# A scheduler's durations refitted, its plan told of two shared PSUM banks, and a rank written out for each of its tasks

## The chip, the cores and the metric

The kernel runs on one core of one Trainium2 chip. The core has five engines with queues of their own: TensorE (PE in the profile, PEld its weight loads), VectorE (DVE), ScalarE (ACT), GpSimd (POOL) and SyncE (SP), which here issues nearly all DMA transfers. Each engine takes its instructions strictly in the order in which they were written into the program and waits on semaphores for what others must have done. The metric is the device time of one execution in microseconds; three runs of the kernel before gave a median of 870.45.

## The reference

An attention block without softmax, with a root-mean-square norm of each head, feeds a two-layer network with softplus:

```python
kv = einsum('bhsd,bhse->bhde', k, v)          # q, k, v: 8 x 8 heads x 576 x 64
out = einsum('bhsd,bhde->bhse', q, kv)
x = out / sqrt(mean(out * out, -1) + 1e-6) * g_norm    # then laid out as 4608 tokens x 512
h = x @ w_in                                   # 512 x 2048
g = log(1 + exp(h))                            # written so that it does not overflow
y = g @ w_out                                  # 2048 x 512; y is 4608 x 512
```

The weights come as 64-bit floats, q, k and v as 32-bit floats.

## The kernel before

**What is computed where.** TensorE multiplies in a 32-bit format that keeps fewer bits than the inputs have, so each operand of the two large products is split into a high part and smaller parts, three pieces in all, and each product is the sum of three matmuls per 128 rows of the contraction. The splitting is ScalarE and VectorE work: for a tile of x, `high` on ACT (L635), `low` (L638) and `less` (L641) on DVE; for the softplus output, L882, L869 and L873 in the first stage and L1117, L1120, L1123 in the later ones.

**The head.** Each 512 KB piece of a 64-bit weight is loaded by SP (L418), turned into 32-bit floats by one ACT instruction (L429) and six DVE instructions (`high1` L433, `high2` L437, `mask` L442, `power` L450, `rest` L455, `total` L459), and split (`low` is L503 or L506, `low_up` L509). For the first four chunks of 128 hidden units the third piece is made with a pair of matmuls (L520 and L521). Meanwhile K and V of the eight batches are loaded (L680, L678) and multiplied in groups of 8 matmuls of 64 columns (L691); q tiles are turned by PE (L771) or, from the third batch, by DVE (L746); an output group (L715, 16 matmuls) makes 128 tokens of attention output; ACT squares them (L788), DVE sums (L719), POOL takes the inverse root with two instructions (L722, L723), DVE scales (L727); the tile is turned by PE (L733) and split into x pieces for block products. Tokens are numbered in 36 tiles of 128, tiles 0 to 2 are block 0, and so on for 12 blocks. The outputs of the attention are also stored to DRAM (L798, L818) and loaded again later (L836, `x_again`). The trace records a group of 32-bit matmuls with two records for each matmul (so the 8 matmuls of L691 stand as x16, the 16 of L715 as x32).

**The first stage.** For each block of 384 tokens and each of the first four or six chunks, a *product* (L858, `mm1`, 12 matmuls of 384 columns) makes the hidden units, ACT applies softplus (L880), ACT and DVE split it, and three groups of three matmuls (L865, `mm2`) add to three sums in PSUM. Attention work is put between these groups until about 300 us.

**The wide stages.** The rest of the hidden units is done in two passes over nine blocks of 512 tokens, two chunks at a time, with seven products (L1060, 6 matmuls of 256 columns) in place of eight. These feed on each other: copies by ACT in PSUM (L1101, L1105, `c1` and `c6` in `wide_step`) stand between a product and a later one that adds to its copy. The second layer is L1130, three matmuls of 512 columns for each of eight places. Sums leave PSUM by ACT (L925), go to DRAM as parts, and come back to be added by DVE (L904).

**What sets the order.** Nothing is ordered by hand. `kernel` creates 3,795 tasks with `add(engine, ns, run, after, pos, take, give, ...)`: an engine, a duration, what must be done before, a position `pos` and the buffers that are taken and given back. `Plan.order` then plays the program: it keeps a clock for each engine and one for the DMA, adds a hand-over time after each task, and again and again takes the task that can start first. Among tasks of one engine that could start within `SOON` (150 ns) of the first, the one with the smallest `pos` wins; PE has rules that keep 64-wide matmuls (kinds `rows` and `kv`) together. The result, sorted by planned start, is the order in which the instructions are written. The chip then runs that order; the planned times themselves are thrown away. `plan.spare` is a filler: where PE would be idle in the plan before the seventh product, a matmul without use (L1224) is put in, 52 in all. `pos` comes from formulas with 179 written numbers (`P0` to `P7`).

```python
at, t = min(options, key=lambda o: (o[1].pos, o[0]))
...
t.start = at
engine_free[t.engine] = at + t.ns
t.end = at + t.ns + self.HANDOVER[t.engine]
```

The buffers `o` (two halves spread over two PSUM banks) and `tp` (one bank) are used by PE, ACT and DVE in turns; the program makes an engine wait until another is done with a bank.

## Time and profile before

| | |
|---|---|
| three runs | 869.46, 870.45 (median), 872.05 us |
| the profiled execution, first to last instruction | 867.5 us; the page gives no other time for it |
| first product L858 starts | 44.44 us |
| last matmul starts | 863.3 us |
| PE busy, of which fillers L1224 | 853.9 us, 18.9 |
| DMA share before the first product | 1.00, 281 GB/s |
| granted clock of TensorE | 1.00 |

The profile comes from one execution, which is 2.95 us shorter in its span than the median run. A row of a timeline has the start, the time from the first start to the last end, the engine, the line, the operation, output and inputs by the program's names, the shape and the number of instructions; brackets hold the idle time of the engine ahead of it and what ended it. Matmuls overlap, so a group's cost is read from its start to the start of the next group.

### The profile page before, as it was taken

What the parts mean: (1) busy time and instruction counts of PE and PEld (TensorE: products, weight loads), DVE (VectorE), ACT (ScalarE), POOL (GpSimd) and SP (SyncE); (2) the same over time, 40 slices, a digit from 0 to 9 for tenths busy, and PEclk for the clock granted to TensorE, in tenths of its full rate; (3) what the DMA queues carried; (4) which work ended last, traced back from release to release, by engine and by line L of the source; (5) the groups of instructions that cost most, each with busy time, mean ns of one, the idle gap of its engine ahead of it and who ended that gap; (6) DMA issues with size and microseconds to landing.
All of it is one profiled execution on the core that took longest, in us unless ns stands there. A gap on an engine that the chain in (4) does not pass through costs nothing.

```text
span 867.5 us, 17041 instructions
## 1 busy us (share of the span) xinstructions
PE 853.9 (98%) x6464; PEld 760.3 (88%) x6464; DVE 704.4 (81%) x995; ACT 521.3 (60%) x980; POOL 76.6 (9%) x79
## 2 busy tenths in 40 slices
PE   7899999999999999999999999999999999999998
PEld 5678888898888999989999999998999899999996
DVE  7888898888788879798887798878788666788873
ACT  6866664445444467766667655654868555566654
POOL 0342223111113200000000000000000000000000
PEclk9999999999999999999999999999999999999999
DMA  9998998779773655436645546545364752777764
GB/s 278 285 242 230 244 262 255 172 224 234 211 188 114 180 175 166 145 108 209 210 156 164 168 151 205 188 144 170 122 201 140 230 165 91 241 236 241 242 190 126
DMA packets 239778, 167.07 MB, mean 193 GB/s; under 512 B 106320, under 2 KB 198736, under 8 KB 239696
## 3 DMA queue, kind: packets, MB, share of 16 engines
q1 hardware_dynamic: 239392, 165.86, 64.5%
q8 instruction: 50, 0.82, 0.4%
q14 instruction: 32, 0.26, 0.1%
q10 hardware_dynamic: 304, 0.13, 0.1%
HBM read 112.98 MB, written 52.95 MB: 191 GB/s over the span
## 4 chain that ended last, share of the span: by engine, by line
PE 94%; DVE 1%; ACT 1%; POOL 0%; issue 0%; ACTq 0%; DVEq 0%
PE banks L1130 31%; PE banks L1060 28%; PE banks L865 16%; PE banks L858 15%; PE banks L715 2%; PE banks L691 2%; PE banks L733 0%; DVE units L638 0%; DVE half L727 0%; PE banks L1224 0%; POOL roots L723 0%; DVE units L641 0%; DVE roots L719 0%; DVE m L459 0%; ACT units L635 0%
## 5 line engine op out<-in xcount | busy, mean ns | idle before, releaser
L1130 PE MATMUL banks<-pieces,gv 128*128 128x512 f32 x768 | 239.9, 394 | 0.0
L1130 PEld LDWEIGHTS banks<-pieces,gv 128*128 128x128 f32 x768 | 133.5, 189 | 18.4
L1130 PE MATMUL banks<-pieces,g_False 128*128 128x512 f32 x384 | 149.4, 389 | 0.0
L858 PE MATMUL banks<-units,pieces 128*128 128x384 f32 x768 | 145.4, 337 | 0.0
L865 PE MATMUL banks<-pieces,gv 128*128 128x512 f32 x576 | 144.9, 396 | 0.0
L858 PEld LDWEIGHTS banks<-units,pieces 128*128 128x128 f32 x768 | 135.5, 188 | 4.8
L865 PEld LDWEIGHTS banks<-pieces,gv 128*128 128x128 f32 x576 | 106.1, 188 | 20.3
L1060 PEld LDWEIGHTS banks<-units,pieces 128*128 128x128 f32 x840 | 112.8, 190 | 6.8 <-ACT banks L1105 0.4
L1060 PE MATMUL banks<-units,pieces 128*128 128x256 f32 x840 | 117.1, 282 | 0.0
L880 ACT ACTIVATE half<-banks 128x384 f32<-128x384 f32 x64 | 31.4, 491 | 98.2 <-PE banks L858 98.0
L1120 DVE TENSOR_TENSOR gv<-g_True,gv 128x1024 fp32r<-128x1024 f32 x47 | 57.5, 1223 | 37.8 <-ACT gv L1117 37.8
L1130 PEld LDWEIGHTS banks<-pieces,g_False 128*128 128x128 f32 x384 | 72.2, 188 | 15.9
L1060 PEld LDWEIGHTS banks<-units,w 128*128 128x128 f32 x504 | 67.8, 190 | 3.9 <-ACT banks L1105 0.2
L1060 PE MATMUL banks<-units,w 128*128 128x256 f32 x504 | 70.7, 282 | 0.0
L723 POOL TENSOR_TENSOR roots<-roots,half 128x8 f32<-128x8 f32 x36 | 62.3, 1731 | 3.0
L1123 DVE SCALAR_TENSOR_TENSOR g_False<-gv 128x1024 fp32r<-128x1024 f32 x47 | 57.6, 1225 | 1.5
L1109 DVE TENSOR_TENSOR g_True<-banks,g_True 128x512 f32<-128x512 f32 x48 | 33.1, 690 | 30.5 <-PE banks L1060 24.5
L1087 ACT ACTIVATE g_True<-banks 128x256 f32<-128x256 f32 x96 | 36.6, 382 | 32.8 <-PE banks L1060 32.2
L1023 DVE TENSOR_TENSOR units<-loads,units 128x1024 fp32r<-128x1024 f32 x42 | 51.2, 1219 | 6.3 <-ACT units L1020 6.3
L925 ACT ACTIVATE m<-banks 128x512 f32<-128x512 f32 x72 | 42.1, 595 | 19.8 <-PE banks L1130 13.8
L1026 DVE SCALAR_TENSOR_TENSOR units<-units 128x1024 fp32r<-128x1024 f32 x42 | 51.4, 1224 | 1.8
L869 DVE TENSOR_TENSOR gv<-half,gv 128x384 fp32r<-128x384 f32 x64 | 35.4, 553 | 20.6 <-ACT gv L882 19.9
(115 smaller groups left out, 1260.5 us busy)
## 6 DMA issues: line engine op xcount, KB each, us to landing
loads<-x SPq DMA_DIRECT2D x180, 128.0 KB, 2.6
part<-m SPq DMA_DIRECT2D x72, 256.0 KB, 2.9
m<-part SPq DMA_DIRECT2D x72, 256.0 KB, 3.2
loads<-form SPq DMA_DIRECT2D x45, 256.0 KB, 3.2
form<-loads SPq DMA_DIRECT2D x36, 256.0 KB, 3.0
raw<-in_moe_w_in_dram SPq DMA_DIRECT2D x16, 512.0 KB, 4.5
loads<-in_k_dram SPq DMA_DIRECT2D x32, 256.0 KB, 4.1
loads<-in_v_dram SPq DMA_DIRECT2D x32, 256.0 KB, 4.4
```

The costliest lines, as they stand in the source:

```text
L723: nc.gpsimd.tensor_tensor(out=r.tile, in0=r.tile, in1=half, op=ALU.pow)
L858: nc.tensor.matmul(hp, lhsT=w_in.tile[:, i, kd * P:(kd + 1) * P], rhs=xv.tile[:, i, kd], start=(m == 0), stop=(m == 3 * KD - 1))
L865: nc.tensor.matmul(mine[i].tile, lhsT=gv.tile[:, m, i * P:(i + 1) * P], rhs=w_out.tile[:, m], start=(c == cs[0] and m == 0), stop=(c == cs ...
L869: nc.vector.tensor_tensor(out=gv.tile[:, 1], in0=g.tile, in1=gv.tile.bitcast(F32)[:, 0], op=ALU.subtract)
L925: a = add("ACT", 690 if ph == LAST else 600, lambda: nc.scalar.activation(new(ot, [P, d_model]), bank.tile, func=AF.Copy, scale=scale if p ...
L1023: nc.vector.tensor_tensor(out=part_of(1, F32R), in0=xl.tile if m > 1 else xl.tile[:, 0], in1=part_of(0), op=ALU.subtract)
L1026: nc.vector.scalar_tensor_tensor(out=part_of(2, F32R), in0=part_of(1), scalar=-RADIX, in1=part_of(0), op0=ALU.mult, op1=ALU.add)
L1060: nc.tensor.matmul(place(q), lhsT=w[:, m, at:at + P], rhs=dst.tile[:, m, v, kd] if u < 6 else dst.tile[:, m, kd], start=(u == 0 and not m ...
L1087: nc.scalar.activation(dst, src, func=AF.Softplus, scale=1.0 + E)
L1120: nc.vector.tensor_tensor(out=gvt(1, F32R), in0=gt(), in1=gvt(0), op=ALU.subtract)
L1123: nc.vector.scalar_tensor_tensor(out=gt(F32R), in0=gvt(1), scalar=-RADIX, in1=gvt(0), op0=ALU.mult, op1=ALU.add)
L1130: nc.tensor.matmul(mine[i].tile, lhsT=(gvt(m, F32R) if m < 2 else gt(F32R))[:, c, i * P:(i + 1) * P], rhs=outs[c].tile[:, m], start=fresh ...
```

## The change

The diff has three parts. The constants of the planner are new: hand-over times, start times, switching costs, the DMA's times, and about 30 task durations; `AHEAD` takes some 0.1 us off each ACT, DVE and POOL task, so that the next task of the engine may start before its end. The planner now knows which tasks touch the banks of `o` and `tp`, and lets a task start there only when the other engines' last planned task in the bank has ended. And `pos` of every task is replaced by its entry in a list, `RANK`, of as many whole numbers as there are tasks. Tasks, their dependencies and their instructions stay the same; only the number of fillers follows the plan, and is 40.

```diff
+RANK = [
+    22, 47, 48, 51, 55, 60, 61, 62, 65, 73, 82, 86, 92, 99, 5, 23, 25, 27, 31, 34, 35, 37, 40, 43, 46, 52, 56, 66, 0, 7, 8, 10, 13, 15, 16, 18, 21, 26,
...
+]
-    HANDOVER = {"PE": 250, "ACT": 120, "DVE": 120, "POOL": 150, "SP": 0}
-    READY = {"PE": 2500, "ACT": 2500, "DVE": 4000, "POOL": 2500, "SP": 700}
-    SWITCH = {("all", "rows"): 90, ("all", "kv"): 90, ("rows", "all"): 250, ("kv", "all"): 250, ("rows", "kv"): 140, ("kv", "rows"): 140}
+    HANDOVER = {"PE": 205, "ACT": 140, "DVE": 121, "POOL": 145, "SP": 0}
+    AHEAD = {"PE": 0, "ACT": 107, "DVE": 88, "POOL": 110, "SP": 0}
+    READY = {"PE": 1600, "ACT": 3250, "DVE": 3050, "POOL": 2500, "SP": 700}
+    SWITCH = {("rows", "rows"): 60, ("all", "kv"): 45, ("rows", "kv"): 45, ("rows", "all"): 112, ("kv", "all"): 118}
+    SHARED = ("o", "tp")
-    LANDING, FILLED = 3500, 60000
+    ENTRY, LANDING, BACKLOG = 1100, 600, 4500
...
-        t = Task(engine, ns, run, [a for a in after if a is not None], pos, list(take), list(give), size)
+        t = Task(engine, ns - self.AHEAD[engine], run, [a for a in after if a is not None], pos, list(take), list(give), size)
...
+        t.banks = {s.ring for s in (*take, *give, *use) if s.ring in self.SHARED}
...
-        dma_free = 1500
+        dma_free = 0
         last_read = {}
+        touched = {b: {} for b in self.SHARED}
...
-                    at = max(engine_free[engine], t.ready)
+                    at = max([engine_free[engine], t.ready, *(end for b in t.banks for e, end in touched[b].items() if e != engine)])
                     if t.size:
-                        at = max(at, dma_free - 2500)
+                        at = max(at, dma_free - self.BACKLOG)
...
+            for b in t.banks:
+                touched[b][t.engine] = t.end
             if t.size:
-                dma_free = max(dma_free, at + t.ns) + t.size
-                t.end = dma_free + (self.LANDING if dma_free > self.FILLED else 2000)
+                dma_free = max(dma_free, at + t.ns + self.ENTRY) + t.size
+                t.end = dma_free + self.LANDING
...
-        f = add("SP", 450, fetch, (), fetch_pos, [raw], size=1800, behind=behind)
+        f = add("SP", 450, fetch, (), fetch_pos, [raw], size=1700, behind=behind)
...
-        a = add("POOL", 2300, root, [a], pos)
+        a = add("POOL", 2180, root, [a], pos)
...
-        c1 = add("ACT", 380, lambda: nc.scalar.copy(place(Y), place(X)), [a1, a5], b + 0.1)
+        c1 = add("ACT", 362, lambda: nc.scalar.copy(place(Y), place(X)), [a1, a5], b + 0.1)
...
     plan.spare = ("h", warm, 400, mm1s[6][1])
+    assert len(RANK) == len(plan.tasks)
+    for t, at in zip(plan.tasks, RANK):
+        t.pos = at
     for t in plan.order():
         t.run()
```

## The prediction

> **What bounds the kernel now.** I read the page first, then the busy time of the engines by stage, then PE's and DVE's timelines of the first 100 us. The page:
>
> ```profile
> span 867.5 us, 17041 instructions
> PE 853.9 (98%) x6464; PEld 760.3 (88%) x6464; DVE 704.4 (81%) x995; ACT 521.3 (60%) x980; POOL 76.6 (9%) x79
> PE   7899999999999999999999999999999999999998
> ```
>
> The second line is busy time by engine, the third PE's busy tenths in 40 slices of 21.7 us. PE is full from the third slice on. The stages say it more sharply (us, busy us of PE, PEld, DVE, ACT, POOL, granted clock, DMA share, GB/s):
>
> ```profile
> 0.00:44.44 44.44, 36.10 (x464) 25.89 (x465) 37.14 (x67) 31.71 (x61) 10.54 (x17) 1.00 1.00 281
> 44.44:80.00 35.56, 34.08 (x441) 28.31 (x440) 30.79 (x53) 22.81 (x46) 13.61 (x13) 1.00 0.92 226
> 80.00:300.00 220.00, 220.00 (x2104) 196.76 (x2103) 188.32 (x323) 111.99 (x223) 52.46 (x50) 1.00 0.78 212
> 300.00:863.50 563.50, 563.50 (x3460) 509.31 (x3458) 447.65 (x553) 354.36 (x652) 0.00 (x0) 1.00 0.56 176
> 863.50:867.50 4.00, 0.21 (x1) 0.00 (x0) 0.48 (x1) 0.47 (x1) 0.00 (x0) 1.00 0.54 200
> ```
>
> From 80 us to the last matmul PE is busy in every microsecond, so no order can gain anything there: it can only lose. What can be gained lies ahead of about 80 us, where DMA (share 1.00) and DVE (37.14 of 44.44) are the full ones. Part of PE's busy time there is filler (L1224) that only runs while nothing else can. PE's timeline shows the marks I count from:
>
> ```profile
> 1.60 5.92 PE L1224 MATMUL banks<-ident_r 128*128 128x512 f32 x13 [1.60 <-DVE ident_r L1184]
> ...
> 42.96 1.65 PE L1224 MATMUL banks<-ident_r 128*128 128x512 f32 x6
> 44.44 2.28 PE L858 MATMUL banks<-units,pieces 128*128 128x384 f32 x12
> ...
> 71.45 2.38 PE L858 MATMUL banks<-units,pieces 128*128 128x384 f32 x12
> ...
> 94.17 2.27 PE L858 MATMUL banks<-units,pieces 128*128 128x384 f32 x12
> ```
>
> These are the first product, the first product of block 1 (the fifth of all) and the first of block 2 (the ninth). Each waits for the x tiles of its block, whose last step is a DVE instruction. DVE's timeline around the first:
>
> ```profile
> 42.31 0.69 DVE L719 TENSOR_REDUCE roots<-half 128x8 f32<-128x512 f32 x1 [0.65 <-ACT half L788]
> 42.91 0.68 DVE L638 TENSOR_TENSOR units<-banks,units 128x512 fp32r<-128x512 f32 x1
> 43.72 0.69 DVE L719 TENSOR_REDUCE roots<-half 128x8 f32<-128x512 f32 x1
> 44.33 0.68 DVE L641 SCALAR_TENSOR_TENSOR units<-units 128x512 fp32r<-128x512 f32 x1
> ```
>
> L638 at 42.91 and L641 at 44.33 finish x tile 2, the last of block 0. Both L719 and the wait of 0.65 in front of them belong to later tiles. So: time = the work PE must do + what PE loses before it never waits again + 4.0 us of tail.
>
> **The change, part by part.** All figures of the changed kernel are places in its built order; durations are the rows of the profile. Every engine issues the same instructions in another order, except that PE has 40 fillers instead of 52; that the change does nothing is therefore excluded. The new numbers in the planner cost nothing themselves.
>
> Fillers: 12 fewer of 0.23 to 0.46 us (5.92 us for 13, 1.65 for 6) is 3 to 5 us of PE time, but in time PE had nothing else to do. Priced at 0; what the waits become is counted below.
>
> PE's price list, start to start in the timeline: a K-V group L691 0.54 (1.08 for 32 matmuls), an output group L715 0.55 (1.09 for 64), a turn L771 or L733 0.41, a pair L520 and L521 0.64, a product L858 2.09, three matmuls of L865 0.693 (2.08 for 9).
>
> 1. Up to the first product. Ahead of it stand 10 K-V groups, 9 q turns, 4 x turns, and before 6 output groups and 5 pairs, after 5 and 6: 17.2 us of work before, 17.3 after. It started at 44.44, so 27.2 us were lost. On DVE, 61 instructions stand before and including the L641 that it needs, after 59: four steps of tiles 3 to 5 (two L719, L638, L641) move behind, one L506 and one L437 move ahead. Two fewer at about 0.65 is 1.3 us. The 0.65 wait belonged to a step that moved behind. On POOL, tile 2's root (two instructions, 1.73 us mean for the second) moves from fourth place to third. SP moves K, V and q loads past weight loads: 6.4 MB instead of 6.7 MB stand up to the last load that the product needs, at 281 GB/s 1 us less, so SP does not forbid the gain. Taken: 44.44 - 1.3 - 0.65 = 42.5. Bounds: 44.44 (a like wait comes back) and 40.0 (DVE's other waits up to there, 0.70 + 0.20 + 0.50 + 0.72 + 0.24 + 0.21, about 2.5, vanish too). I stay near the first, since those wait for ACT and weight loads that are ahead as before.
>
> 2. From there to block 1. PE work in between, after: 5 K-V groups, 1 q turn, 2 pairs, 5 output groups, 4 x turns, 4 products, 12 threes of L865 = 25.5 (before 23.8 in 27.0 us). So PE cannot start block 1 before 42.5 + 25.5 = 68.0. DVE: the fifth product's last input is DVE's 104th instruction in the new order (72nd in the old, where the product waited for PE's own stream). In the old run instructions 62 to 104 took 28.5 us with 3.5 us of visible waits, 25.0 for 43, 0.58 each. New: the 59th ends near 43.1, plus 45 x 0.58 = 69.2. The product starts 0.57 ahead of that end, as the first did (44.44 against 45.01), since it reads this third last: 68.6. DVE's waits in this stretch: bounds 0 and the old 3.5; taken 0.5, because between a tile's L719 and its L727, where POOL works, the new order mostly leaves 2.7 us of other DVE work, which is what the last such tile took (L719 at 55.83 to L727 at 59.19, less 0.69). Block 1 at 69.1.
>
> 3. To block 2. PE work after: 18.4 (2 K-V groups, 2 output groups, 4 turns, 4 products, 9 threes), 87.5. DVE: 134 instructions up to its last input in both orders, so 30 more; the old run took 20.5 with 1.8 of waits, 0.62 each; with fewer instructions directly behind the one that they read (38 instead of 47) I take 0.60, 18.0. Waits: 1.0 for one tile whose L727 follows its L719 too closely, and 0.5 for the last x load of block 2, which on SP now has 21.9 MB up to it instead of 19.2 (it landed at 76.82; 2.7 MB more at 226 to 281 GB/s is 9.6 to 12, so 86 to 89, just when DVE gets there). 69.7 + 18.0 + 1.5 - 0.57 = 88.6; bounds 86.4 (PE alone, from 68.0) and 91.9 (all the old waits). Work ahead of it: 62.6 before, 61.2 after. Lost: before 94.17 - 62.6 = 31.6, after 27.4. Gain 4.2.
>
> 4. From block 2 to 300 us. PE goes 23 times instead of 21 from large matmuls to 64-wide ones, 23 instead of 21 back, 11 instead of 10 between the two small kinds; a change costs 0.095, 0.14 and 0.13 in the spacing of the old run's matmuls. Plus 0.6. Waits there: none before, and the new order leaves more work between a product and what reads its result. Priced 0 for that, covered by 31.7 us of idle DVE; with that cover gone, each microsecond DVE is late is one of PE's.
>
> 5. The wide stages (300 to 863.5). Places where only one group of PE work stands between a product L1060 and the product that needs its copy: 4 before, 25 after. PE's and ACT's timelines show the chain: product at 837.09, copy L1105 38.00 to 38.36, next product at 838.50, exactly behind the three matmuls between. No such place lost PE time before. Taken 0; bounds 0 and 25 x 0.60 (one L925 of 595 ns in ACT's queue ahead of each copy) = 15.
>
> Sum: 4.2 - 0.6 = 3.6 us. The profiled execution's span is 867.5, so 863.9; the median of the runs, 870.45, is 2.95 longer, which I keep: **866.8**.
>
> One rule speaks against fewer fillers. Row: 13 fillers took 5.92 us at the start, later 6 took 1.65, while the clock row reads 1.00 throughout; the longest PE wait afterwards was 1.7 (L691 for K). The Trainium skill, "TensorE: Matmul & The Clock Gate", Part 1, says that PE starts at half rate and drops back to it after some 3.4 us of idleness; by it, a longer wait in the new head would slow what follows. The time is rival four.
>
> **The rivals.** *The waits move along.* DVE keeps all waits of the old run: 3.5 in part 2, 1.8 more in 3. Then block 2 starts at 91.9 (43.1 + 26.1 + 3.5 + 18.0 + 1.8 - 0.57), 30.7 lost, gain 0.9 - 0.6: 870.1. For it: an in-order queue hands a wait on. Against: four waits in part 2 were L727 behind a close L719.
> *More than forecast.* The DVE waits before the first product vanish as well, 2.5, and PE alone bounds after it (2.2): 866.8 - 4.7 = 862.1. Against: DMA share 1.00.
> *Slower.* In the wide stages ACT's queue holds the copies up at the 25 tight places. At 0.4 each 10 us: 876.8. It turns the sign when the mean passes 3.6 / 25 = 0.14. For it: L925 leaves the sums in just those stretches (72 of them). Against: the four old places cost nothing.
> *The clock falls.* Three waits over 3 us in the head, each followed by as long at the half pace of the first fillers: 3 x 1.7 = 5.1, 871.9.
>
> **How the numbers follow.** Forecast (863.5 to 869) 0.47; waits move along 0.16; more 0.18; slower 0.16; clock 0.03. A measurement here tells 0.3% (2.6 us) from no change. Faster: 0.47 without its upper edge (0.02), plus 0.18, 0.63. Same: 0.16 + 0.02 + 0.02, 0.20. Slower 0.17. The range leaves out a tenth at each side: 860.5 (rival two with 1.5 us more) to 873.
>
> **What would show it.** First L858 at 42 to 43, the fifth at 69 to 70, the ninth at 88 to 89; PE full from 88 on; DVE without the 0.65 wait ahead of tile 2; in 300 to 863 no PE wait on ACT banks L1101 or L1105. Wrong if DVE's 104th instruction ends after 72 us, or if the wide stages take longer than before.

## The result: slower by 0.6%

The changed kernel takes 875.16 us (median of 7 runs, 871.77 to 879.18), the kernel before beside it 870.08 (7 runs, 869.01 to 872.05): a ratio of 1.0058, 95% interval 1.0038 to 1.0079, so 5 us more. The forecast of 866.8 and the end of its range, 873.0, both lie below. The runs also scatter over 7.4 us where the kernel before scatters over 3.

The profiled execution, A below, took 879.18 us, the most of the seven (span 877.4), so its 9.9 us over the span before are twice the median loss. The same order was profiled once more, execution B (`after_again`, 871.87 us, the least of its five, span 870.1). The page of A:

```profile
span 877.4 us, 16991 instructions
PE 856.3 (98%) x6452; PEld 758.9 (86%) x6452; DVE 697.5 (79%) x995; ACT 515.6 (59%) x980; POOL 80.4 (9%) x79
PE   7799999999999999999999999999999999999997
```

These busy shares are within two points of those of before and do not say where the time went. The stages, cut at the first product, of A and then of B (columns as before: us, PE, PEld, DVE, ACT, POOL, granted clock, DMA share, GB/s):

```profile
0.00:49.83 49.83, 36.65 (x424) 26.43 (x425) 36.94 (x66) 30.56 (x59) 10.14 (x15) 0.93 0.89 244
49.83:80.00 30.17, 30.14 (x371) 26.13 (x370) 27.80 (x49) 21.56 (x43) 12.71 (x12) 1.00 0.88 229
80.00:300.00 220.00, 218.43 (x2178) 194.04 (x2177) 183.65 (x321) 111.98 (x225) 57.54 (x53) 1.00 0.80 215
300.00:872.30 572.30, 570.63 (x3483) 512.24 (x3483) 448.63 (x559) 350.49 (x654) 0.00 (x0) 1.00 0.56 175
872.30:877.40 5.10, 0.48 (x3) 0.06 (x1) 0.48 (x1) 1.00 (x2) 0.00 (x0) 0.85 0.39 133
```

```profile
0.00:45.34 45.34, 34.13 (x424) 24.21 (x425) 36.45 (x66) 30.11 (x59) 10.75 (x15) 1.00 0.95 267
80.00:300.00 220.00, 219.77 (x2131) 195.35 (x2130) 185.30 (x326) 112.10 (x225) 56.40 (x52) 1.00 0.79 211
300.00:865.00 565.00, 564.63 (x3455) 507.28 (x3454) 442.88 (x548) 346.62 (x645) 0.00 (x0) 1.00 0.56 175
865.00:870.08 5.08, 0.47 (x3) 0.05 (x1) 0.48 (x1) 0.99 (x2) 0.00 (x0) 0.99 0.39 132
```

Two things to see. The head has DMA shares of 0.89 and 0.95 instead of 1.00, and A has a clock of 0.93. And PE, which before was busy in every microsecond from 80 us to the last matmul, is not any more: 1.57 and 1.67 us of idleness behind 80 us in A, 0.23 and 0.37 in B. That is a cost in the place where the prediction said that an order can only lose.

**A common measure.** To compare orders I take PE's lost time: the start of a matmul, less the median spacing of all matmuls ahead of it (by line, fillers left out, spacings from the trace of before; some 815 us up to the last one). It grows where PE waits. How it drifts from stretch to stretch in the kernel before (it falls by 2.8 us behind 350 us) depends on the medians, so only differences between kernels are read from it. The tail is what comes behind the last matmul's start.

| execution | first product | ninth | lost at first, ninth, 300 us | 350 us to last matmul | tail | span |
|---|---|---|---|---|---|---|
| before | 44.44 | 94.17 | 29.6, 36.3, 51.1 | -2.8 | 4.16 | 867.5 |
| changed, A | 49.83 | 96.30 | 34.4, 39.8, 56.6 | +0.8 | 5.01 | 877.4 |
| changed, B | 45.34 | 91.90 | 29.9, 35.4, 51.3 | -1.2 | 5.01 | 870.1 |

B is 0.3 us behind at the first product, has gained 0.9 us at the ninth, has lost it again by 300 us, and then loses 1.6 us in the wide stages and 0.85 in the tail. A is 4.8 us behind at the first product already, 5.5 at 300 us, and loses 3.6 and 0.85 later. So there are two losses: one in the head, which comes and goes, and one behind 350 us, which is always there.

**The wide stages.** The waits of TensorE's matmuls and weight loads behind 350 us, changed kernel (A; us in total, times, longest):

```profile
PE banks L1215 <- ACT g_True L1239: 0.9, 1, 0.9
PE banks L1285 <- DVE banks L1059: 0.5, 1, 0.5
PE banks L1215 <- DVE g_True L1264: 0.2, 1, 0.2
PEld banks L1215 <- ACT g_True L1239: 2.3, 6, 1.1
PEld banks L1215 <- ACT banks L1256: 1.5, 8, 0.2
PEld banks L1215 <- ACT g_True L1242: 1.0, 3, 0.5
```

Before, the same answer has a single line, `PEld banks L1060 <- ACT banks L1105: 0.6, 3, 0.2`. The longest gaps in the spacing of the matmuls are at 408.6 us (1.1), 791.4 (0.35), 822.3 (0.2) and 830.7 us (0.64). The timeline of the first and of the last:

```profile
407.15 0.68 ACT L584 ACTIVATE sq<-raw 128x512 bf16<-128x512 bf16 x1 [3.14 <-DMA raw<-in_moe_w_in_dram]
407.73 0.59 ACT L1080 ACTIVATE m<-banks 128x512 f32<-128x512 f32 x1
408.21 0.37 ACT L1239 COPY g_True<-banks 128x256 f32<-128x256 f32 x1
408.63 0.97 PE L1215 MATMUL banks<-early,w 128*128 128x256 f32 x6 [0.95 <-ACT g_True L1239]
...
829.92 0.70 DVE L1059 TENSOR_TENSOR banks<-m,m 128x512 f32<-128x512 f32 x1 [1.83 <-DMA m<-part]
...
830.68 0.73 PE L1285 MATMUL banks<-pieces,gv 128*128 128x512 f32 x2 [0.48 <-DVE banks L1059]
```

In the first, ACT stands for 3.14 us at the conversion of a weight piece whose load has not landed, and the copy that a product needs is queued behind it. In the last, DVE waits 1.83 us for a partial result, and TensorE needs that very sum. The four gaps are 2.3 of the 3.6 us that A loses here. In B there are two, of 0.22 and 0.47 us at 815.1 and 823.4 us, 0.7 of 1.6. So in each about 1 us is left in small losses of under 0.2 us.

**The tail.** The last output tile is split between ACT and DVE so that two short stores end the kernel. The new order puts a whole tile behind it: ACT issues a DMA that waits for DVE, and only then copies that tile.

```profile
872.14 0.47 ACT L1070 ACTIVATE m<-banks,scale 128x256 f32<-128x256 f32 x1 [1.35 <-PE banks L1285]
872.65 0.48 DVE L1073 TENSOR_SCALAR m<-banks,scale 128x256 f32<-128x256 f32 x1 [5.60 <-ACT m L1070]
873.62 0.69 ACT L1080 ACTIVATE m<-banks,scale 128x512 f32<-128x512 f32 x1 [1.01 <-DVE m L1073]
874.34 0.35 SPq L1095 DMA_DIRECT2D out_dram<-m  x1
```

**The head.** Stretches of 5 us around the first product, changed kernel, A:

```profile
40.00:45.00 5.00, 2.85 (x41) 2.35 (x43) 4.38 (x9) 3.28 (x7) 3.09 (x3) 0.80 0.90 209
45.00:50.00 5.00, 5.00 (x64) 4.14 (x61) 1.98 (x4) 1.57 (x3) 0.00 (x0) 0.51 0.86 237
```

TensorE waits 1.51 us for V ahead of 41.20 and 0.81 ahead of 44.09, and from 43.0 to 49.9 us it runs at half the clock (a K-V group takes 1.12 us instead of 0.69). DVE waits 2.99 us for a group's result. In B the clock reads 1.00 throughout the head. The same groups in the same order, from that K-V group to the first product, take 5.74 us in A (44.09 to 49.83) and 3.21 in B (42.13 to 45.34): of the 4.5 us by which A's first product is behind B's, the low clock is 2.5.

The other cost of the head is in A and B alike. DVE converts the weights, and the new order puts more loads of q, K and V ahead of the weight loads: SP issues the second and fourth of these at 3.2 and 11.8 us before, at 4.8 and 16.5 in B. DVE's waits for weights up to 44 us, before and then B (us in total, times, longest):

```profile
DVE m L433 <- DMA raw<-in_moe_w_in_dram: 1.3, 1, 1.3
DVE m L433 <- DMA g<-in_moe_w_out_dram: 0.5, 1, 0.5
```

```profile
DVE m L589 <- DMA g<-in_moe_w_out_dram: 2.6, 2, 1.5
DVE m L589 <- DMA raw<-in_moe_w_in_dram: 1.8, 2, 1.6
```

That is 1.8 us before and 4.4 in B; A has 5.0.

### The profile page after: what moved, and what is told of

It reads as the page before. It is cut to its first block, busy times and chain, and to the rows that moved or that the text cites. A ratio compares the mean times of both kernels' runs of the same rounds, so it can differ in the third digit from the quotient of the medians.

```text
span 877.4 us, 16991 instructions
## 1 busy us (share of the span) xinstructions
PE 856.3 (98%) x6452; PEld 758.9 (86%) x6452; DVE 697.5 (79%) x995; ACT 515.6 (59%) x980; POOL 80.4 (9%) x79
## 4 chain that ended last, share of the span: by engine, by line
PE 89%; DMA 7%; DVE 2%; ACT 1%; SPq 1%; issue 1%; ACTq 0%; DVEq 0%
PE banks L1285 28%; PE banks L1215 26%; PE banks L1013 15%; PE banks L1020 15%; PE banks L870 2%; PE banks L846 2%; DMA loads<-in_v_dram 2%; DMA raw<-in_moe_w_in_dram 1%; DMA loads<-in_k_dram 1%; DMA m<-part 1%; PE banks L888 1%; DMA g<-in_moe_w_out_dram 1%; DMA loads<-form 0%; DMA w<-in_q_dram 0%; DVE units L1178 0%
## 5 line engine op out<-in xcount | busy, mean ns | idle before, releaser
L1285 PE MATMUL banks<-pieces,gv 128*128 128x512 f32 x768 | 239.9, 394 | 0.5 <-DVE banks L1059 0.5
L1285 PEld LDWEIGHTS banks<-pieces,gv 128*128 128x128 f32 x768 | 133.5, 189 | 19.1 <-DVE banks L1059 0.9
L1285 PE MATMUL banks<-pieces,g_False 128*128 128x512 f32 x384 | 149.5, 389 | 0.0
L1013 PEld LDWEIGHTS banks<-units,pieces 128*128 128x128 f32 x768 | 135.1, 188 | 5.3 <-ACT half L1035 0.3
L1215 PE MATMUL banks<-units,pieces 128*128 128x256 f32 x804 | 112.0, 283 | 0.1
L1215 PEld LDWEIGHTS banks<-units,pieces 128*128 128x128 f32 x804 | 106.2, 190 | 6.4 <-ACT g_True L1239 0.6
L1285 PEld LDWEIGHTS banks<-pieces,g_False 128*128 128x128 f32 x384 | 72.2, 188 | 15.9
L1215 PE MATMUL banks<-units,w 128*128 128x256 f32 x480 | 68.4, 283 | 0.0
L1215 PEld LDWEIGHTS banks<-units,w 128*128 128x128 f32 x480 | 63.9, 190 | 4.2 <-ACT banks L1256 0.6
L878 POOL TENSOR_TENSOR roots<-roots,half 128x8 f32<-128x8 f32 x36 | 64.5, 1792 | 3.0
L1035 ACT ACTIVATE half<-banks 128x384 f32<-128x384 f32 x64 | 31.2, 487 | 54.2 <-PE banks L1013 39.7
L1178 DVE TENSOR_TENSOR units<-loads,units 128x1024 fp32r<-128x1024 f32 x40 | 48.9, 1222 | 13.9 <-ACT units L1175 13.7
L1080 ACT ACTIVATE m<-banks 128x512 f32<-128x512 f32 x72 | 42.0, 593 | 16.8 <-PE banks L1285 8.6
L1181 DVE SCALAR_TENSOR_TENSOR units<-units 128x1024 fp32r<-128x1024 f32 x40 | 48.9, 1222 | 2.5 <-DVE units L1178 0.5
L1272 ACT ACTIVATE gv<-g_True 128x1024 fp32r<-128x1024 f32 x47 | 49.8, 1060 | 1.2
L1175 ACT ACTIVATE units<-loads 128x1024 fp32r<-128x1024 f32 x40 | 42.4, 1060 | 12.5 <-DMA loads<-form 6.4
```

Of the source, the lines that this page charges most:

```text
L878: nc.gpsimd.tensor_tensor(out=r.tile, in0=r.tile, in1=half, op=ALU.pow)
L1013: nc.tensor.matmul(hp, lhsT=w_in.tile[:, i, kd * P:(kd + 1) * P], rhs=xv.tile[:, i, kd], start=(m == 0), stop=(m == 3 * KD - 1))
L1080: a = add("ACT", 690 if ph == LAST else 600, lambda: nc.scalar.activation(new(ot, [P, d_model]), bank.tile, func=AF.Copy, scale=scale if p ...
L1175: nc.scalar.activation(part_of(0, F32R), xl.tile if m > 1 else xl.tile[:, 0], func=AF.Copy, scale=DOWN)
L1178: nc.vector.tensor_tensor(out=part_of(1, F32R), in0=xl.tile if m > 1 else xl.tile[:, 0], in1=part_of(0), op=ALU.subtract)
L1181: nc.vector.scalar_tensor_tensor(out=part_of(2, F32R), in0=part_of(1), scalar=-RADIX, in1=part_of(0), op0=ALU.mult, op1=ALU.add)
```

## Experiments

All but two kernels fix the order outright. `RANK` holds each task's place in one sequence, fillers included, and an engine takes its tasks only in that sequence; instructions and buffers are the changed kernel's. With the changed kernel's own sequence this is the changed kernel (`after_again`). Lines of these kernels stand one to three higher than those of the changed kernel (L1286 is its L1285).

```diff
+        queue = {e: sorted((t for t in self.tasks if t.engine == e), key=lambda t: t.pos) for e in self.READY}
...
+                    if t is not queue[engine][0]:
+                        continue
...
-                if best is None or at < best[0]:
+                if best is None or t.pos < best[1].pos:
...
-        return sorted(done, key=lambda t: t.start)
+        return done
```

Below, `before` and `after` are the two sequences, with the starts that their plans give. The lines with `sequence` tell an edit in words; in the kernels it is the list `RANK` that differs.

### Which stretch of the order costs the time

```diff
-sequence = after
+sequence = [t in before that start ahead of 48.36] + [the rest as in after]     # before_to_first_then_after
+sequence = [t in after that start ahead of 41.76] + [the rest as in before]     # after_to_first_then_before
+sequence = [t in before that start ahead of 346.5] + [the rest as in after]     # before_to_wide_then_after
+sequence = [t in after that start ahead of 305.6] + [the rest as in before]     # after_to_wide_then_before
```

> Every engine follows the kernel before up to its first product of a block step (L858 there), and the changed kernel's order from there; the instructions are the same. Theory A, 'the head': the changed kernel loses its time ahead of the first product (49.83 against 44.44 us in the two profiled executions, 5.4 us) and nothing behind it: first product at 44 to 45 us and 868 to 871 us in all, no more than the kernel before. Theory B, 'the wide stages': the order of the wide stages costs what the trace of the changed kernel shows behind 300 us (PE's start less the work ahead of it grows by 2.6 us from 300 us to the last matmul, against 0.2 before, and the tail is 0.9 longer): 872.5 to 874 us, although the head is the one of before.

> The mirror of it: the changed kernel's order up to its first product, that of the kernel before from there. Theory A: first product at 49 to 50 us, and the 5.4 us stay to the end: 874.5 to 876.5 us. Theory B: the head's loss is made good while products wait for nothing, the wide stages are those of before: 870 to 872 us.

> The kernel before up to its first product of a wide stage (L1089 there, about 300 us), the changed kernel's order from there. Theory A: 869.5 to 871 us, as before. Theory B: 872.5 to 874.5 us, with PE waits of over 0.5 us behind 380 us as in the changed kernel.

> The mirror: the changed kernel up to the first product of a wide stage, the order of before from there. Theory A: 874.5 to 876.5 us, no PE waits of over 0.5 us behind 380 us. Theory B: 871 to 872.5 us. Were both only parts of the truth, the four runs would add up: the differences of this run and of its mirror from the kernel before would sum to the changed kernel's 5.1 us.

Measured, in ratios to the kernel before: 1.0052 (1.0037 to 1.0067), 1.0057 (1.0040 to 1.0074), 1.0105 (1.0090 to 1.0120) and 1.0030 (1.0021 to 1.0040), that is +4.7, +5.3, +9.6 and +2.8 us. Neither theory is right alone: the changed order costs with the head of before, and the head costs with the order of before behind it. The expected sum doesn't hold either (9.6 + 2.8 is not 5.1), and the trace shows why: a seam has a price. In the third kernel TensorE waits once for 3.4 us right at the seam (its waits in 330 to 350 us):

```profile
PE banks L1015 <- ACT half L1037: 3.4, 1, 3.4
```

So the totals are bounds, and I read the stretches away from the seams. From 350 us to the last matmul every profiled execution with the order of before has -2.8 or -2.9 (six of six, the kernel with fourteen more tight places left out). Those with the changed order have +0.8, -1.2, +0.3, +0.1, +0.7, +1.0 and +3.1 (`q_loads_later` and the two filler kernels below among them), and all a tail of 4.96 to 5.01 instead of 4.16. The wide stages therefore cost 1.6 to 5.9 us, 3.5 in the middle, and the tail 0.8.

A later run tried to place that loss:

```diff
-sequence = after
+sequence = [t in before that start ahead of 642.2] + [the rest as in after]
```

> The kernel before up to the first product of the second phase of its wide stages, the changed kernel's order from there (some 240 us and the tail). If the loss lies where the traces of the changed order show gaps in most executions (785 to 831 us, 0.5 to 1.2 us, some 0.5 us of small waits, and 0.85 us in the tail): 871.3 to 873 us, with the head and the clock of the kernel before. If it lies in the first phase (a gap of 1.1 us at 408 us in one execution): 869.5 to 870.8 us, that is the tail alone.

Measured: 881.95 us, ratio 1.0144 (1.0127 to 1.0161), outside both expectations, and again by a seam, here of 6.9 us at 640 us (TensorE's waits behind 330 us):

```profile
PE banks L1217 <- ACT banks L1258: 6.9, 1, 6.9
PE banks L1287 <- DVE banks L1061: 1.5, 1, 1.5
```

Behind the seam, from 650 us on, the lost time rises by 1.6 us to the last matmul where it falls by 1.4 before; the second line is the wait for a partial result at 833 us that the changed kernel has at 830. So the second phase alone has about 3.0 us of the loss in this execution, and the tail its 0.8.

### Is the plan's landing time the cause?

Behind 330 us a load of A really takes 2.6 to 4.6 us from issue to landing in the median of its kind and 5.2 to 6.3 at worst. For a partial result (`m<-part`) it is 3.4 and 6.3; with no other transfer ahead, the constants of the old plan allow such a load 4.75 us (350 + 900 + 3500 ns), those of the new one 2.95 (350 + 1100 + 900 + 600), which is below the median.

```diff
-    ENTRY, LANDING, BACKLOG = 1100, 600, 4500
+    ENTRY, LANDING, BACKLOG = 1100, 2500, 4500      # landing_2500
...
-                t.end = dma_free + self.LANDING
+                t.end = dma_free + (2500 if dma_free > 60000 else self.LANDING)      # landing_2500_behind_60
```

> The changed kernel with one constant of its plan changed: a load counts as landed 2500 ns behind the queue instead of 600, so its consumers are placed 1.9 us later in the order of their engines; ranks, durations and bank waits stay. Theory C, 'no margin': behind 330 us the real time from issue to landing is 2.0 to 4.4 us in the median and 4.9 to 6.3 us at worst for the kinds of loads, the changed kernel's plan allows 2.8 to 4.2, that of the kernel before 4.3 to 5.9; where a landing is late, the in-order engine that waits for it holds up work that PE needs (four PE gaps of 0.2 to 1.1 us behind 345 us, 2.3 us in all, and some 1.1 us of small ones; the kernel before has none). With 1.9 us more of allowance the gaps go: 870.5 to 872.5 us. Theory D, 'the ranks' (the order itself is worse, whatever the plan's landing): gaps stay, 874 to 877 us.

> The same constant only behind 60 us of the plan; up to there the changed kernel's 600. Theory C: the wide stages lose their gaps, the head stays as in the changed kernel (first product at 47 to 50 us, clock below 1.00 in 40 to 55 us): 871 to 873 us. Theory D: 874 to 877 us. Against the run before it tells what the allowance is worth in the head.

Both kernels return a wrong result (a relative error of 0.045), so they are read for time alone. Measured: 891.87 us (1.0252, 1.0228 to 1.0277) and 884.91 (1.0184, 1.0144 to 1.0225), 10 to 17 us slower than the changed kernel. The second gained nothing in the wide stages either (+2.4 from 350 us). With other landing times the ranks, which were fitted to one plan, give another order everywhere: the second loses 3.5 us more between 300 and 350 us, and in 80 to 330 us its products wait for x tiles (L790, L793) and for ACT's reading of an earlier product (L1035). TensorE's waits there, the first three of five rows:

```profile
PE banks L1013 <- ACT units L790: 2.4, 2, 1.6
PE banks L1013 <- ACT half L1035: 1.8, 1, 1.8
PE banks L1013 <- DVE units L793: 0.8, 2, 0.4
```

Theory C isn't supported in this form; the runs don't settle whether the thin allowance made the ranks bad in the first place. One by-product mattered: the second kernel has the changed kernel's head, and its first product starts at 44.79 us with the clock at 1.00.

### The head: the clock, the fillers, the first loads

```diff
-sequence = after
+sequence = after with 16 fillers ahead of five groups in 36 to 47 us       # after_16_fillers
+sequence = after with 45 fillers, ahead of each group as many as it waits  # after_full_fillers
+sequence = after                                                            # after_again
+sequence = before without its last 12 fillers                               # before_40_fillers
+sequence = before without fillers                                           # before_no_fillers
```

> The changed kernel with sixteen more idle products (L1379), put where its PE waited in 36 to 47 us: the rest of the order is the same. Theory E, 'the clock': granted clock 0.80 and 0.51 in 40 to 50 us came from those waits and cost 2.5 to 3 us; with the fillers the clock stays at 1.00, first product at 45.5 to 47.5 us, 872 to 874 us. If the loads alone set the first product: clock at 1.00 or not, first product still 47.5 to 50 us, 874.5 to 877 us.

> The changed kernel with 45 more idle products (85 instead of 40), as many ahead of each group of TensorE as its wait there would hold at full clock by the two executions in which the clock did not fall; the rest of the order is the same. Theory E2, 'the clock decides between two heads': with no wait of over 0.5 us left the clock stays at 1.00, the first product comes at 44.5 to 45.5 us in every execution, the slow half of the changed kernel's runs goes: median 2 to 3 us under after_again, highest less lowest under 4 us. If loads and buffers alone make the two heads and the clock only follows: no gain over after_again, the spread stays.

> The changed kernel's order once more, beside the others on the same chip: 873 to 876 us, first product at 44.7 us with the clock at 1.00 or at 47.4 to 49.8 us with a clock below 1.00 in 40 to 56 us.

> The kernel before without the last 12 of its 52 idle products, those that stand in 36 to 48 us of its plan: as many as the changed kernel has. The prediction priced that at nothing. Theory E2: TensorE then waits 1 to 1.5 us at a stretch in 33 to 44 us, the clock falls in some executions, and these lose 2 to 5 us: median 0 to 3 us over the kernel before, highest less lowest over 4 us. If the prediction's price was right: 869 to 870.5 us, and the spread of before (some 2.5 us).

> The kernel before without any of its 52 idle products. Theory E2: the clock stays low through much of the head, where TensorE then waits some 12 us in all; the first product at 47 to 52 us, 873 to 878 us. If the clock doesn't matter in the head: 869 to 870.5 us.

| kernel | us (runs) | ratio, 95% | first product | clock in the head |
|---|---|---|---|---|
| after_16_fillers | 877.56 (875.90 to 878.24) | 1.0084, 1.0057 to 1.0110 | 48.38 | 0.67 in 24 to 28 us |
| after_full_fillers | 877.30 (876.74 to 878.01) | 1.0089, 1.0075 to 1.0103 | 47.12 | 1.00 |
| after_again | 874.00 (871.87 to 874.72) | 1.0047, 1.0034 to 1.0061 | 45.34 | 1.00 |
| before_40_fillers | 868.68 (867.80 to 870.56) | 0.9993, 0.9983 to 1.0003 | 43.04 | 0.68 in 8 to 12 us |
| before_no_fillers | 871.53 (869.40 to 872.28) | 1.0018, 1.0008 to 1.0028 | 45.94 | 0.50 to 0.91 in 16 to 36 us |

A clock at 1.00 does not bring the first product back, so the low clock is a part of A's loss and not its root. With 85 fillers it stays at 1.00, the scatter shrinks to 1.3 us as expected, and the kernel is 3.3 us slower than `after_again`, not 2 to 3 faster. And on the kernel before, two thirds of the clock for 20 us cost 2 us in all (`before_no_fillers`):

```profile
16.00:36.00 20.00, 14.61 (x239) 11.84 (x240) 15.91 (x28) 14.04 (x29) 3.82 (x4) 0.66 0.96 283
```

(columns as in the stages.) TensorE has room there, so most of the lost speed comes out of waiting; in A it stood right ahead of the first product, with nothing to wait for, and 6.8 us at half the clock cost 2.5. Twelve fillers fewer cost nothing, as the prediction said.

What then? The seven executions that keep the changed order up to the first product have it at 44.70, 44.79, 44.81, 45.34, 47.41, 47.75 and 49.83 us; the four that keep the order and the fillers of before through it have it at 43.75 to 44.44. In the seven, DVE waits 3.2 to 5.3 us for weights ahead of the first product and SP issues the fourth weight load at 15.9 to 16.7 us; in six that keep the order of before up to there it waits 1.5 to 2.2 us, and the load is issued at 11.8 to 12.3. Loads land later, too: the 45th DMA (not the same load in the two orders) at 41.0 to 44.3 us in the seven, at 38.3 to 40.2 in the six. The seven part early among themselves: the 31st DMA lands at 28.6 to 28.7 us where the first product comes at 44.7 or 44.8, at 29.2 where it comes at 45.34 and also where it comes at 47.41, at 30.1 for 47.75, and at 31.0 in A, well ahead of the fall of A's clock at 43.0 us (and at the first product at 47.41 the clock was still at 1.00). The four K and V buffers tie the engines together: SP may load when TensorE has read a buffer, and TensorE can work when SP has loaded. A late landing goes round that loop: in the chain that leads to A's first product, TensorE has read a pair of buffers at 35.7 us, SP issues the next K and V at 36.4 and 36.9, V lands 7.04 us later, and TensorE goes on at 44.09. That extra fillers go round it as well is my reading; no run shows it. What makes the same order's loads land later in one execution than in another isn't settled. The early DMA rates of before and of B:

```profile
0.00:5.00 5.00, 3.40 (x8) 2.72 (x9) 2.19 (x9) 1.92 (x2) 0.69 (x6) 1.00 0.59 174
5.00:20.00 15.00, 12.00 (x106) 7.96 (x106) 13.07 (x23) 9.71 (x19) 0.60 (x1) 1.00 1.06 320
```

```profile
0.00:5.00 5.00, 1.22 (x2) 0.50 (x2) 1.96 (x8) 1.65 (x2) 0.73 (x7) 1.00 0.50 144
5.00:20.00 15.00, 12.74 (x77) 9.03 (x78) 11.86 (x20) 9.71 (x21) 0.20 (x1) 1.00 0.95 264
```

The changed kernel loads q first, each tile in two DMAs, and moved 264 GB/s in 5 to 20 us instead of 320. So I moved q back:

```diff
-sequence = after
+sequence = after, four loads of q (L916), their transposes (L926) and copies (L933) 6 us later
```

> The changed kernel with the first four loads of q (L916, each two DMAs), their transposes (L926) and the copies behind them (L933) put 6 us later in the orders of SP, TensorE and ACT; K, V and the weights go first, as in the kernel before; all else stays. Theory H, 'q first starves the rest': in five executions of the changed order the 45th DMA landed at 41.3 to 44.3 us, in four of the order before at 38.7 to 40.2, and 271 and 276 GB/s were moved in 5 to 15 us against 333 and 317; with q later the loads of K, V and weights land 1 to 2 us earlier, the first product comes at 44 to 47 us: 873 to 874.5 us. If the order of the first loads doesn't matter: first product at 47 to 50 us, 874.5 to 877 us.

Measured: 882.69 us (881.98 to 885.50), ratio 1.0159 (1.0138 to 1.0181), first product at 54.98: 8.7 us more than `after_again`, the other way round from theory H. In 20 to 30 us DMA was busy for 0.43 and DVE for 2.44 of 10 us:

```profile
20.00:30.00 10.00, 6.83 (x40) 4.99 (x40) 2.44 (x5) 4.25 (x8) 0.00 (x0) 0.83 0.43 125
```

Every engine keeps its queue in order, so what was moved back by 6 us held up what now stood behind it. One half of theory H did come: the fourth weight load is issued at 13.7 us, DVE's waits for weights fall to 1.8 us, as in the kernel before, and in 10 to 20 us DVE is busy for 8.42 us (before: 8.32). So the early q loads did make the weights late. But from 20 us on DVE waits for ACT, 9.2 us for conversions and 4.9 for squares: one kind of instruction can't be moved in this head alone.

### The wide stages: data that comes late, or tight places?

```diff
-sequence = after
+sequence = after, ACT's and DVE's work on loaded data up to 2.5 us later       # wide_consumers_later
+    and the loads 2 us earlier, and the last whole tile ahead of the split one  # wide_all_three
+    and the q loads as in the run above                                         # q_later_and_wide_all
```

> The changed kernel's order with one kind of move behind its first wide stage: what ACT and DVE do to freshly loaded data (weights L584 to L597, units L1175 to L1181, the additions of partial results L1059; 432 instructions) is put up to 2.5 us later in the order of its engine, never closer than 0.6 us ahead of what needs it. TensorE's and SP's orders are not touched. Theory F, 'in-order queues held by late loads': ACT L584 waited 3.1 us for its load at 407 us and held the copies behind it (PE lost 1.1), ACT L1175 waited 3.5 us at 787 us (PE lost 0.35), DVE L1059 1.8 us at 830 us (PE lost 0.64); with the moves these gaps and most of the 1.1 us of small waits go, the tail stays: 2 to 3 us less than the changed kernel, 872 to 873.5 us. Theory G, 'the loads themselves are late' (whoever waits, the product behind needs that data): the gaps stay or move to PE itself, 874.5 to 876.5 us.

> The same moves, and two more: the loads of the wide stages stand 2 us earlier in SP's order (319 of them, ahead of stores), and at the very end the last output tile that ACT copies whole (L1080) stands ahead of the one that is split (L1070, L1073), with TensorE's last two groups exchanged, as in the kernel before. Theory F: all of the 4.0 us that the wide stages and the tail took goes, tail 4.2 us instead of 5.0: 871 to 872.5 us, which leaves the head's part. Theory G: only the tail's 0.8 us and what earlier loads bring: 873.5 to 875 us.

> All moves of the last two together. If theories F and H both hold, their gains add: 868.5 to 871 us, level with the kernel before or ahead of it. If only F: 871 to 872.5; if only H: 872.5 to 874.5; if neither: 874 to 877 us.

Measured: 906.28 us (1.0427, 1.0396 to 1.0458), 931.31 (1.0726, 1.0688 to 1.0765) and 939.19 (1.0806, 1.0787 to 1.0825): 31 to 64 us slower than the changed kernel, a miss of every expectation. I had left out that whoever reads loaded data later frees its buffer later. SP's waits in 350 to 860 us, `wide_consumers_later`, and the changed kernel:

```profile
SPq L1126 <- DVE units L1179: 102.3, 33, 7.6
SPq L1096 <- ACT m L1081: 45.6, 27, 4.7
SPq L1126 <- DVE turned L1179: 34.0, 15, 6.4
```

```profile
SPq L1125 <- DVE units L1178: 70.8, 27, 6.3
SPq L1095 <- ACT m L1080: 54.8, 26, 7.0
```

SP waits 102.3 instead of 70.8 us for DVE to free the unit buffers, so the next load starts later by as much and the wait for it comes back. Loads that stand earlier in SP's queue wait there for the same buffers, with the stores behind them. Theory F, a queue held by a late load, is what the timelines above show, but its cure by lateness is none, and G isn't tested by these runs.

One suspect can be tested where nothing else is in the way. The prediction counted places with one group of TensorE between a product and the product that needs its copy, 4 before and 25 after. I made such places in the kernel before:

```diff
-sequence = before
+sequence = before, with 14 groups of three L1130 moved from ahead of a product L1060 to behind it
```

> The kernel before with fourteen groups of three matmuls L1130 moved from ahead of a product L1060 to behind it, so that 18 products instead of 4 have one group between them and the product whose copy (L1105) they read; nothing else moves. The changed kernel's trace shows 0.2 us of waiting of the weight loads at each such place and up to 0.1 us of lost spacing of the matmuls. If that is their price: +1 to +2.8 us, 870.5 to 872 us, and the start of PE less the work ahead of it falls by 0.8 to 1.8 us from 350 us to the end instead of 2.8. If the prediction's price, nothing, was right: 869 to 870 us, a fall of 2.8, and the loss of the wide stages is in the few long gaps. If the rival's 0.4 us each: 875 us.

Measured: 869.35 us (11 runs, 868.79 to 870.85), ratio 0.9998 (0.9989 to 1.0007). The weight loads do wait (TensorE's weight loads in 350 to 870 us):

```profile
PEld banks L1217 <- ACT banks L1262: 3.4, 17, 0.3
```

3.4 us instead of 0.6, yet the matmuls lose 0.5 us in all (-2.3 from 350 us instead of -2.8), 0.04 at a place. By that price the 21 more tight places of the changed kernel are some 0.8 us, an estimate. They are thus about the small losses that were left over above, and a fifth of A's loss in the wide stages but half of B's; the rest is in the gaps, in which ACT or DVE come late by more than a group's length. That late loads make these gaps is read from the timelines; no run here removes them.

### Can the gain at the ninth product be kept?

```diff
-sequence = before
+sequence = before to its first product, after to its eighth (78.8 us of its plan), the rest as in before
```

> The kernel before up to its first product, the changed kernel's order for its first two blocks (to the eighth product), the kernel before from there. In the splice that kept the changed kernel's order to the end, PE's start less the work ahead of it stood at 33.6 us at 75 us, against 35.2 in the kernel before, and at 37.0 against 36.6 at 100 us. If that gain of 1.6 us can be kept: 867.5 to 868.5 us; if the switch back takes it again, as it was taken by 100 us there: 869 to 871 us.

Measured: 871.24 us (869.16 to 873.20), ratio 1.0018 (1.0005 to 1.0032). Lost time at the ninth product 38.4 us against 36.3: the switch back took more than the gain. No kernel here beats the kernel before; `before_40_fillers` comes nearest, and its interval includes 1.

## Why the prediction was wrong, step by step

- **What bounds the kernel** was right: PE is full from 80 us on, so an order can gain only ahead of it and lose behind. The sum used the first half alone.
- **Part 1, the first product at 42.5, failed.** It came at 44.70 to 45.34 in four executions and at 47.41 to 49.83 in three. The step that failed is "SP does not forbid the gain". It summed the bytes up to the last load that the product needs and divided them by the old rate of 281 GB/s (the changed order reaches 267 and 244), and it took the weight loads to be "ahead as before", though q, K and V move past them. The weights that DVE converts ahead of that product come later, and DVE waits for them 1.0 to 3.8 us longer than before (3.2 to 5.3 us instead of 1.5 to 2.2), where two instructions fewer and the wait of 0.65 were to save 1.95. The DVE instruction that was to end near 43.1 (its 59th, without the six that set up constants) ended at 44.6 to 46.2. In A TensorE itself came later still, behind the late V load and at half the clock. Even the bound of 44.44 was missed.
- **Part 2, 1.1 us lost up to block 1, held**: 27.29 and 26.71 us from the first to the fifth product (72.63 and 76.54), less the 25.5 of work, are 1.8 and 1.2, against 3.2 before. This is the one gain that came.
- **Part 3** held in its length: 19.3 and 19.8 us to the ninth product, forecast 19.5. Gain 0.2 and -0.3, forecast 0.
- **Part 4** was a little small: the lost time grows by 15.9 and 16.8 from the ninth product to 300 us, by 14.8 before, so 1.1 to 2.0 instead of 0.6.
- **Part 5, the wide stages at 0, is the other large miss**: 1.6 to 5.9 us. The tight places cost little (0.04 us each, some 0.8 for 21 more), but they were the only thing looked at. Not looked at were the places where ACT and DVE wait for loads that hold up what TensorE needs; in the timelines the two longest gaps of A, 1.1 and 0.64 us, are there.
- **The tail** was kept at 4.0 without looking at its order, and took 0.85 more.
- **The rivals.** "Slower" named the right stages and the right sign, with 876.8 near the 875.2 measured, but by luck: its mechanism was the copies of tight places at 0.4 each, of which 0.04 was measured. "The clock falls" happened, at waits half as long as it asked for; in A it came behind late loads. Its price was put too high, 1.7 us for every 3 or so: 6.8 us at 0.50 cost A 2.5 us, and 0.66 of the clock over 20 us cost 2 us where TensorE had waits to spare. "The waits move along" put the ninth product at 91.9, where B has it (91.90), but that is luck: it had the first product at 42.5 and the waits behind it, and B lost its time ahead of the first.
- **The signs of being wrong** both came: DVE's 104th instruction ends at 72.1 us in B and 76.0 in A, against a limit of 72, and the wide stages take longer. Of the signs of being right, one held: no matmul of A or B shows a wait behind 300 us for the copies that are L1101 and L1105 in the kernel before.
- **The chances** gave 0.17 to slower. Three of the five parts were about the head, where the gain was to be; the 560 us of wide stages, where only losses are possible, were looked at for one kind of place and taken at 0.

Together, in B: -0.3 at the first product, +1.2 by the ninth, -1.1 by 300 us, -1.6 in the wide stages, -0.85 in the tail, 2.6 us of loss. By the prediction's own prices for the groups the first two terms are -0.8 and +1.7, with the same sum. The median of the changed kernel lies 2 to 3 us above that, with later heads and longer gaps.

## What to carry to other kernels

Where one engine is full for most of the span, a new order is judged by the stretches where it can only lose: for every instruction that waits for a load there, look at what is queued behind it and who needs that. A wait of the weight loads or a tight place has almost no price by itself (0.04 us here); count gaps in the spacing of the matmuls. Where loads are moved ahead of others in an in-order queue, ask who reads those that now come later: here DVE waited up to 3.8 us longer for weights. And before moving the reader of a loaded buffer, ask when the buffer comes free: 2.5 us of patience cost 31 us here.

## What the runs showed of the hardware that I had not expected

- In A the granted clock reads 1.00 in 42.0 to 43.0 us, 0.54 in 43.0 to 43.5 and 0.50 from there to 48.0. The wait of 1.51 us had ended at 41.20, and the wait of 0.81, up to 44.09, came behind the fall. A wait of 2.98 us ahead of 5.80 left the clock at 1.00. The Trainium skill, "TensorE: Matmul & The Clock Gate", Part 1, puts the drop behind an idle window of about 3.4 us. This trace does not agree if that is read as one unbroken wait: the clock fell after shorter waits, and a longer one left it up. What sets the fall off is not shown here.
- What a low clock costs depends on who waits. Without any filler TensorE was at 0.50 to 0.91 of its clock for 20 us, and the kernel lost 2.06 us (0.18%) with TensorE busy for 14.61 of the 20; in A, with TensorE busy without a break, 5.74 us at 0.50 were 3.21 us of work.
- Weight loads that wait 3.4 us over 17 places cost TensorE 0.5 us.
